# Moving one slab's skip term from TensorE to VectorE in a fused state-space and gated-FFN block, with four smaller shifts of loads and order

## The chip, the cores and the metric

One core of one Trainium2 chip runs the whole program. The metric is device time in microseconds (us) of one execution. The kernel before took 184.93 us (median of four executions beside the changed kernel, 184.4 to 185.17), a span of 183.4 us on the profile. PE is TensorE, PEld its weight loads, DVE VectorE, ACT ScalarE, POOL GpSimd, SP SyncE. L469 is line 469 of the kernel in question; the changed kernel's lines lie a few further down, so the instructions at L469 there are at L471 or so here.

## The reference

```python
xn = layernorm(x)                          # x: 2048 tokens x 512, no scale or bias
# A: diagonal state-space model, 512 complex states
Lam_bar = exp(dt * Lam);  B_bar = ((Lam_bar - 1) / Lam)[:, None] * B
h_t = Lam_bar * h_(t-1) + B_bar xn_t
y = 2 * Re(C h) + xn * Dskip               # the skip term
# B: gated FFN, F = 1376
f = (gelu(xn @ w_gate) * (xn @ w_up)) @ w_down
out = x + y * silu(f)
```

## The kernel before

The tokens are worked off in four slabs of 512 (NS = 4), each of four tiles of 128 (M = 4). Per slab, TensorE makes gate and up (eleven blocks of F), the u product of the state-space model, the down projection (`f_ps`, 11 matmuls a tile) and y (`y_ps`, 8 matmuls a tile). VectorE makes the gated products `at` (two blocks of F at a time, block 10 alone; blocks are counted from 0), the rotation by the complex phase (`pp`, `qq`, their combinations `Wt` and `hst`), the scans `Ft`, and the epilogues. The y of a slab is made during the next slab's FFN, that of the last slab at the end.

The skip term takes one of two ways. Where a tile is in `zs` (in the kernel before all tiles of slabs 1 and 2 and the first two of slab 3), VectorE makes `z = xn * Dskip` and adds it to y in the epilogue; elsewhere TensorE adds it with four small matmuls on a diagonal matrix.

```python
    def y_mm(s, m, hst):
        for h in range(2):
            flush(("h", s, h))
        y_ps = psum.tile([P, D], FP32, name="y_ps", tag="ps")
        for j in range(2 * NPT):
            nc.tensor.matmul(y_ps[:, :], lhsT=hst[:, j // NPT, j % NPT, m0 : m0 + P],
                             rhs=C2[:, j // NPT, j % NPT, :], ...)
        for kt in range(0 if (s, m) in zs else KT):          # skip term on TensorE
            nc.tensor.matmul(y_ps[:, kt * P : (kt + 1) * P], lhsT=xnT[:, kt, mg : mg + P],
                             rhs=diagI[:, kt, :], ...)
    # [...]
    def epi(s, m, y_ps, g2):
        def f():
            y = y_ps
            if (s, m) in zs:                                  # skip term on VectorE
                y = work.tile([P, D], FP32, name="yt", tag="tt", bufs=3)
                TT(out=y[:], in0=y_ps[:, :], in1=zs[s, m][:], op=ALU.add)
            TT(out=yg[:], in0=y[:, :], in1=g2[:], op=ALU.mult)
            TT(out=ot[:], in0=yg[:], in1=x_tok[:, s * M + m, :], op=ALU.add)
        dve(now() + 0.3, 1.6 if (s, m) in zs else 0.95, f)
    # [...]
    def skip(s, m, xn):
        zs[s, m] = work.tile([P, D], BF16, name="z", tag="z", bufs=9)
        dve(now() + 1.5, 0.34, lambda: TT(out=zs[s, m][:], in0=xn[:], in1=Db[:], op=ALU.mult))
```

The order of VectorE's instructions is fixed when the kernel is built, from modelled clocks: `later` puts rotation and scans in a waiting list; `dve` first takes from that list whatever the model says can still be finished in time, then emits its own instruction; `flush` takes out what a following matmul needs.

```python
    def drain(t, late):
        while waiting and max(clk["dve"], waiting[0][0]) + waiting[0][1] <= t + late:
            pop()

    def dve(ready, cost, f, late=0.8):
        drain(ready, late)
        clk["dve"] = max(clk["dve"], ready) + cost
        f()
    # [...] in ffn, after each pair of blocks:
            dve(now() + lag, 0.61, lambda: TT(out=at[:, j - 1 : j + 1, :], in0=gt[:], in1=ub[:], op=ALU.mult))
    # [...] the last slab:
    y0 = y_mm(s, 0, hsts[s])
    for m in range(M):
        g2s[s, m] = down(s, m, ats[s])
        if m == 0:
            epi(s, 0, y0, g2s[s, 0])
```

Of the kernel before, what the change touches and what calls it, by code (L numbers as in the profile page):

```python
# [19 lines left out]
def kernel(  # L20
# [70 lines left out]
    for i, v in enumerate((A_log_dt, A_Lambda_im, A_Lambda_re, A_Dskip)):  # L91
        nc.scalar.dma_start(out=pv[4 * i : 4 * i + 4, :], in_=v.rearrange("(k p) -> k p", p=P))
    CUTS = (0, 3 * P, 8 * P, F)

    def load_gu(i):
        a, b = CUTS[i], CUTS[i + 1]
        nc.sync.dma_start(out=wg[:, :, a:b], in_=wg_r[:, :, a:b])
        nc.sync.dma_start(out=wu[:, :, a:b], in_=wu_r[:, :, a:b])
# [8 lines left out]

    load_gu(0)
    load_x(1)
    load_gu(1)  # L110
    load_x(2)
    nc.sync.dma_start(out=Db[:], in_=A_Dskip.unsqueeze(0).to_broadcast([P, D]))
    for h in range(2):
        for ri, src in enumerate((A_B_re, A_B_im)):
            for pt in (h * H2, h * H2 + 1):
                nc.sync.dma_start_transpose(
                    out=BT[:, ri, :, pt * P : (pt + 1) * P], in_=src[pt * P : (pt + 1) * P, :]
                )
    load_gu(2)

# [80 lines left out]

    bn(0, 0)
    bn(0, 1)
    bn_end(0, 0)
    bn_end(0, 1)
    rstd(0, 0, 2)
    nc.gpsimd.tensor_tensor(out=dt_[:], in0=euler[:], in1=ldt, op=ALU.pow)
    bn(0, 2)
    bn(0, 3)
    xs = [norm0(0), norm0(1)]  # L210
    bn_end(0, 2)
    bn_end(0, 3)
    rstd(0, 2, 4)
    tps = [t_xn0(0, xs[0]), t_xn0(1, xs[1])]
    xnT_out(nc.vector, 0, tps[0])
    xnT_out(nc.scalar, 1, tps[1], 0, KT // 2)
    xnT_out(nc.vector, 1, tps[1], KT // 2, KT)
    xs += [norm0(2), norm0(3)]
    SPLIT = 2
    early = {}  # L220
# [15 lines left out]

    for j in range(SPLIT):
        for up in range(2):
            early[j, up] = gu_mm(0, j, up, 0, TS // 2)
        if j == 0:  # L240
            tps += [t_xn0(2, xs[2]), t_xn0(3, xs[3])]
            xnT_out(nc.scalar, 3, tps[3])
    STT(out=thn[:], in0=lim, scalar=1.0 / (2.0 * math.pi), in1=dt_[:], op0=ALU.mult, op1=ALU.mult)
# [115 lines left out]
    U0_AT = (5, 7)  # L359
    Y_AT = {1: (5, 7, 9, 10), 2: (1, 2, 3, 4), 3: (2, 4, 6, 8)}  # L360

# [141 lines left out]
    def epi(s, m, y_ps, g2):  # L503
        mg = s * TS + m * P
        yg = work.tile([P, D], BF16, name="yg", tag="yg")
        ot = work.tile([P, D], BF16, name="ot", tag="ot")

        def f():
            y = y_ps
            if (s, m) in zs:  # L510
                y = work.tile([P, D], FP32, name="yt", tag="tt", bufs=3)
                TT(out=y[:], in0=y_ps[:, :], in1=zs[s, m][:], op=ALU.add)  # L512
            TT(out=yg[:], in0=y[:, :], in1=g2[:], op=ALU.mult)  # L513
            TT(out=ot[:], in0=yg[:], in1=x_tok[:, s * M + m, :], op=ALU.add)

        dve(now() + 0.3, 1.6 if (s, m) in zs else 0.95, f)
        nc.sync.dma_start(out=out_td[mg : mg + P, :], in_=ot[:])

    def y_halves(s, m, hst, g2):
        m0 = m * P  # L520
        mg = s * TS + m0
        yg = work.tile([P, D], BF16, name="yg", tag="yg")
        ot = work.tile([P, D], BF16, name="ot", tag="ot")
        for i in range(2):
            c = slice(i * D // 2, (i + 1) * D // 2)
            y_ps = psum.tile([P, D // 2], FP32, name="y_ps", tag="ps")
            for j in range(2 * NPT):
                nc.tensor.matmul(
                    y_ps[:, :], lhsT=hst[:, j // NPT, j % NPT, m0 : m0 + P], rhs=C2[:, j // NPT, j % NPT, c],
                    start=(j == 0), stop=False,  # L530
                )
            for kt in range(KT // 2):
                k = i * (KT // 2) + kt
                nc.tensor.matmul(
                    y_ps[:, kt * P : (kt + 1) * P], lhsT=xnT[:, k, mg : mg + P], rhs=diagI[:, k, :],
                    start=False, stop=(kt == KT // 2 - 1),
                )
            TT(out=yg[:, c], in0=y_ps[:, :], in1=g2[:, c], op=ALU.mult)
            TT(out=ot[:, c], in0=yg[:, c], in1=x_tok[:, s * M + m, c], op=ALU.add)
            (nc.sync, nc.scalar)[i].dma_start(out=out_td[mg : mg + P, c], in_=ot[:, c])  # L540
# [28 lines left out]
    def skip(s, m, xn):  # L569
        zs[s, m] = work.tile([P, D], BF16, name="z", tag="z", bufs=9)  # L570
        dve(now() + 1.5, 0.34, lambda: TT(out=zs[s, m][:], in0=xn[:], in1=Db[:], op=ALU.mult))  # L571

# [8 lines left out]

    clk["pe"] = 8.1
    clk["dve"] = 10.3
    hsts, ats, g2s = {0: hst0}, {0: at0}, {}
# [18 lines left out]
    ln_vector_small(1)  # L603
    dve(13.0, 2.8, lambda: ln_vector(2))
    later(14.0, 1.2, lambda: TT(out=v4(t2_[:]), in0=v4(sa[:]), in1=sB, op=ALU.mult))
    later(14.0, 1.2, lambda: TT(out=v4(t1_[:]), in0=v4(ca[:]), in1=cB, op=ALU.mult))
# [5 lines left out]
    for s in range(NS):  # L612
        for j in range(NFT):
            ffn(s, j, ats[s])
            if s == 0:
# [9 lines left out]
                if j == 2 + M:  # L625
# [6 lines left out]
                    load_c(1)  # L632
                    load_x(3)
                if j in U0_AT:
                    chain(0, U0_AT.index(j), u_pair(0, U0_AT.index(j)), hst0)
            else:
                if j in Y_AT[s]:
                    m = Y_AT[s].index(j)
                    epi(s - 1, m, y_mm(s - 1, m, hsts[s - 1]), g2s[s - 1, m])
                if s < NS - 1 and 1 <= j < 1 + M:  # L640
                    ln_out(s + 1, j - 1)
        if s < NS - 1:
# [13 lines left out]
    s = NS - 1  # L656
    y0 = y_mm(s, 0, hsts[s])
    for m in range(M):
        g2s[s, m] = down(s, m, ats[s])
        if m == 0:  # L660
            epi(s, 0, y0, g2s[s, 0])
    for m in range(1, M - 1):
# [32 lines left out]
```

## Time and profile before

| | kernel before |
|---|---|
| device time | 184.93 us |
| span in the profile | 183.4 us |
| TensorE busy | 177.8 us (97%) |
| VectorE busy | 163.5 us (89%) |
| granted clock of TensorE | 1.0 |

Four parts of the page answer most of the question: the busy time of each engine, the row of tenths with the granted clock, the chain of waits that ended last, and the list of what each engine waited for. From the page of the kernel before, three rows of the second part (the span in 40 slices; each digit is the busy share or the granted clock in tenths), and the chain's shares by engine:

```profile
PE   7899999999999999999999999999999999999992
DVE  4886999999997999999999999999999999996053
PEclk9999999999999999999999999999999999999999
...
PE 87%; DMA 4%; DVE 4%; ACT 2%; SPq 1%; issue 0%; DVEq 0%
```

TensorE has no gap worth naming after its start, and never loses its clock there. VectorE has hardly more between slice 5 and slice 36. The busy time by stage says how few (the view of windows of the kernel before: window, length, then busy time and number of instructions of each engine, and the mean granted clock):

```profile
core 0: us, PE busy (x) PEld busy (x) DVE busy (x) ACT busy (x) POOL busy (x), PEclk, DMA share, GB/s
...
15.40:161.50 146.10, 145.95 (x688) 67.04 (x687) 143.06 (x205) 99.90 (x173) 11.18 (x23) 1.00 0.24 53
161.50:169.00 7.50, 7.50 (x36) 3.55 (x35) 6.27 (x12) 3.46 (x5) 0.00 (x0) 1.00 0.09 29
```

In the 146 us of the main part TensorE is busy for 145.95 and VectorE for 143.06.

### The profile page before, as it was taken

How to read it: one execution, taken by the hardware profiler on the slowest of the kernel's cores; microseconds unless marked ns; L12 is line 12 of the kernel's file. 1: busy time of each engine (PE TensorE's matmuls, PEld its weight loads, DVE VectorE, ACT ScalarE, POOL GpSimd, SP SyncE). 2: the span in 40 equal slices, each digit the busy share in tenths (PEclk: the TensorE clock that was granted, in tenths of full speed). 3: DMA queues.
4: the chain of work that ended last, by engine and by line, in shares of the span. 5: the costliest groups of instructions: out<-in, count | busy, mean ns of one | idle time of the engine just before them, and what ended most of it. 6: DMA issues, size and time to landing. Idle time of an engine off the chain costs nothing.

```text
span 183.4 us, 2452 instructions
## 1 busy us (share of the span) xinstructions
PE 177.8 (97%) x863; PEld 83.7 (46%) x863; DVE 163.5 (89%) x258; ACT 112.8 (62%) x196; POOL 19.9 (11%) x44
## 2 busy tenths in 40 slices
PE   7899999999999999999999999999999999999992
PEld 2474444544444444544444444444444444454451
DVE  4886999999997999999999999999999999996053
ACT  3189997678899855257789665667529444371210
POOL 3667601800000000000003000000000000000000
PEclk9999999999999999999999999999999999999999
DMA  5999695596001410010000132200000000000002
GB/s 147 309 373 120 110 225 108 129 301 168 3 0 29 80 35 32 0 45 12 0 4 0 32 84 57 57 5 0 0 0 0 0 32 29 0 30 29 29 4 86
DMA packets 24588, 12.39 MB, mean 68 GB/s; under 512 B 15776, under 2 KB 24576, under 8 KB 24576
## 3 DMA queue, kind: packets, MB, share of 16 engines
q1 hardware_dynamic: 24400, 12.16, 27.9%
q8 instruction: 7, 0.11, 0.3%
q10 hardware_dynamic: 176, 0.07, 0.1%
q14 instruction: 5, 0.04, 0.1%
HBM read 6.46 MB, written 2.10 MB: 47 GB/s over the span
## 4 chain that ended last, share of the span: by engine, by line
PE 87%; DMA 4%; DVE 4%; ACT 2%; SPq 1%; issue 0%; DVEq 0%
PE f_ps L476 21%; PE up_ps L230 19%; PE g_ps L230 19%; PE u_ps L375 15%; PE y_ps L491 13%; DMA wu<-in_B_w_up_dram 3%; DMA out_dram<-ot 1%; ACT gt L463 1%; ACT ub L464 1%; ACT xn L575 1%; DVE hst L395 1%; SPq L90 1%; DVE qq L391 1%; PE y_ps L496 0%; DVE z L571 0%; DVE yg L513 0%
## 5 line engine op out<-in xcount | busy, mean ns | idle before, releaser
L230 PE MATMUL g_ps<-xnT,wg 128*128 128x512 bf16 (+2 forms) x184 | 45.6, 370 | 0.5 <-ACT xnT L198 0.5
L230 PE MATMUL up_ps<-xnT,wu 128*128 128x512 bf16 (+2 forms) x184 | 45.5, 370 | 0.3 <-DMA wu<-in_B_w_up_dram 0.3
L463 ACT ACTIVATE gt<-g_ps 128x512 bf16<-128x512 f32 (+1 forms) x44 | 26.9, 611 | 21.1 <-PE g_ps L230 21.0
L476 PE MATMUL f_ps<-wd,at 128*128 128x512 bf16 (+1 forms) x176 | 38.7, 379 | 0.0
L464 ACT ACTIVATE ub<-up_ps 128x512 bf16<-128x512 f32 (+1 forms) x44 | 27.0, 614 | 8.0 <-PE up_ps L230 8.0
L421 DVE TENSOR_TENSOR_SCAN Ft<-rho,it,Wt 128x512 bf16<-128x512 f32 x24 | 29.6, 1269 | 0.0
L491 PE MATMUL y_ps<-C,hst 128*128 128x512 bf16 x120 | 28.4, 379 | 0.1
L375 PE MATMUL u_ps<-xnT,BT 128*128 128x512 bf16 x128 | 28.4, 379 | 0.0
L230 PEld LDWEIGHTS <-wu 128*128 128x128 bf16 (+1 forms) x184 | 18.3, 100 | 20.1 <-DMA wu<-in_B_w_up_dram 0.6
L230 PEld LDWEIGHTS <-wg 128*128 128x128 bf16 (+1 forms) x184 | 18.2, 100 | 19.5 <-issue 0.5
L476 PEld LDWEIGHTS <-at 128*128 128x128 bf16 (+1 forms) x176 | 17.2, 98 | 20.9
L380 ACT ACTIVATE U<-u_ps 128x512 bf16<-128x512 f32 x32 | 19.0, 614 | 8.6 <-PE u_ps L375 8.2
L481 ACT ACTIVATE g<-f_ps 128x512 f32<-128x512 f32 x16 | 9.6, 597 | 16.3 <-PE f_ps L476 16.3
L375 PEld LDWEIGHTS <-BT 128*128 128x128 bf16 x128 | 12.5, 98 | 14.8
L491 PEld LDWEIGHTS <-hst 128*128 128x128 bf16 x120 | 11.6, 98 | 14.5 <-DVE hst L395 0.6
L469 DVE TENSOR_TENSOR at<-gt,ub 128x1024 bf16<-128x1024 bf16 x20 | 13.5, 676 | 0.0
L512 DVE TENSOR_TENSOR yt<-y_ps,z 128x512 f32<-128x512 f32 x10 | 6.8, 680 | 7.1 <-PE y_ps L491 7.1
L157 DVE BATCH_NORM_STATS2 st<-x_tok 128x6 f32<-128x512 bf16 x12 | 7.5, 682 | 4.0 <-DMA x_tok<-in_A_x_dram 3.9
L395 DVE TENSOR_TENSOR hst<-pp,qq 128x1024 bf16<-128x1024 bf16 x16 | 10.6, 687 | 0.2
L395 DVE TENSOR_TENSOR Wt<-pp,qq 128x1024 bf16<-128x1024 bf16 x16 | 10.4, 685 | 0.2
L575 ACT ACTIVATE xn<-x_tok,nb,rs 128x512 bf16<-128x512 bf16 x12 | 10.3, 856 | 0.0
L391 DVE TENSOR_TENSOR pp<-U,cos_b 128x2048 bf16<-128x2048 bf16 x8 | 9.8, 1223 | 0.4
(109 smaller groups left out, 155.7 us busy)
## 6 DMA issues: line engine op xcount, KB each, us to landing
out_dram<-ot SPq DMA_DIRECT2D x15, 128.0 KB, 1.7
x_tok<-in_A_x_dram SPq DMA_DIRECT2D x3, 512.0 KB, 7.3
wd<-in_B_w_down_dram SPq DMA_DIRECT2D x1, 1280.0 KB
wg<-in_B_w_gate_dram SPq DMA_DIRECT2D x1, 640.0 KB
wu<-in_B_w_up_dram SPq DMA_DIRECT2D x1, 640.0 KB, 9.6
wg<-in_B_w_gate_dram SPq DMA_DIRECT2D x1, 384.0 KB, 4.4
wu<-in_B_w_up_dram SPq DMA_DIRECT2D x1, 384.0 KB
wg<-in_B_w_gate_dram SPq DMA_DIRECT2D x1, 352.0 KB
```

The costliest lines, as they stand in the source:

```text
L230: nc.tensor.matmul(ps[:fs, a:b], lhsT=w[:, kt, fsl], rhs=xnT[:, kt, s * TS + a : s * TS + b], start=(kt == 0), stop=(kt == KT - 1),)
L375: nc.tensor.matmul(u_ps[:, :], lhsT=BT[:, ri, kt, pt * P : (pt + 1) * P], rhs=xnT[:, kt, cols], start=(kt == 0), stop=(kt == KT - 1),)
L380: ACT(out=U[:, ri, q, :], in_=u_ps[:, :], func=AF.Copy)
L391: TT(out=box[key][:], in0=src()[:], in1=tab[:, hs, :].unsqueeze(1).to_broadcast(W), op=ALU.mult)
L395: return lambda: TT(out=dst()[i], in0=box["pp"][:, i, :, :], in1=box["qq"][:, 1 - i, :, :], op=op)
L421: nc.vector.tensor_tensor_scan(out=box["F"][:, ri, q, :], data0=rho[:, pt : pt + 1].to_broadcast([P, TS]), data1=box["W"][:, ri, q, :], in ...
L463: ACT(out=gt[:fs, i, :], in_=g_ps[:fs, :], func=AF.Gelu_apprx_tanh)
L464: ACT(out=ub[:fs, i, :], in_=u_ps[:fs, :], func=AF.Copy)
L469: dve(now() + lag, 0.61, lambda: TT(out=at[:, j - 1 : j + 1, :], in0=gt[:], in1=ub[:], op=ALU.mult))
L476: nc.tensor.matmul(f_ps[:, :], lhsT=at[:fs, k, m0 : m0 + P], rhs=wd[:fs, k, :], start=(k == 0), stop=(k == NFT - 1))
L491: nc.tensor.matmul(y_ps[:, :], lhsT=hst[:, j // NPT, j % NPT, m0 : m0 + P], rhs=C2[:, j // NPT, j % NPT, :], start=(j == 0), stop=((s, m) ...
L575: ACT(out=xn[:], in_=x_tok[:, s * M + m, :], func=AF.Identity, scale=rs[:, s, m : m + 1], bias=nb[:, s, m : m + 1])
```

## The change

The intent is to take sixteen small matmuls (the skip term of slab 0) off TensorE, the engine with 97%. Their z has no room of its own, so it is kept in the part of `x_tok` where the last slab's x will be, and that x is loaded later. With it come a start with norms one by one and weights in four loads instead of three, y of slabs 0 and 1 a step later, a third buffer for the output tile, and y of the last slab's first tile behind the third down projection rather than ahead of the first.

```diff
-    CUTS = (0, 3 * P, 8 * P, F)
+    CUTS = (0, 2 * P, 5 * P, 8 * P, F)
@@ loads
     load_gu(0)
+    load_gu(1)
     load_x(1)
-    load_gu(1)
+    load_gu(2)
     load_x(2)
@@ start: statistics, norms and copies of slab 0
-    bn(0, 0)
-    bn(0, 1)
-    bn_end(0, 0)
-    bn_end(0, 1)
-    rstd(0, 0, 2)
+    for m in range(2):
+        bn(0, m)
+        bn_end(0, m)
+        rstd(0, m, m + 1)
     [...]
-    xnT_out(nc.vector, 0, tps[0])
+    xnT_out(nc.scalar, 0, tps[0])
     [...]
-    SPLIT = 2
+    SPLIT = 3
@@ when y and the next x's norm are made
-    Y_AT = {1: (5, 7, 9, 10), 2: (1, 2, 3, 4), 3: (2, 4, 6, 8)}
+    Y_AT = {1: (6, 8, 9, 10), 2: (2, 3, 4, 5), 3: (2, 4, 6, 8)}
+    XN_AT = {1: 1, 2: 2}
@@ epi, y_halves
-        ot = work.tile([P, D], BF16, name="ot", tag="ot")
+        ot = work.tile([P, D], BF16, name="ot", tag="ot", bufs=3)
@@ skip
-        zs[s, m] = work.tile([P, D], BF16, name="z", tag="z", bufs=9)
+        if s == 0:
+            z = x_tok[:, (NS - 1) * M + m, :]
+        else:
+            z = work.tile([P, D], BF16, name="z", tag="z", bufs=9)[:]
+        zs[s, m] = z
@@ after the statistics of slab 2
+    for m in range(M):
+        skip(0, m, xs[m])
@@ main loop
-                    load_x(3)
     [...]
+        if s == 1:
+            load_x(3)
@@ last slab
-    y0 = y_mm(s, 0, hsts[s])
     for m in range(M):
         g2s[s, m] = down(s, m, ats[s])
-        if m == 0:
-            epi(s, 0, y0, g2s[s, 0])
+        if m == 2:
+            epi(s, 0, y_mm(s, 0, hsts[s]), g2s[s, 0])
```

More of the change, by code (lines that the diff above doesn't have):

```diff
@@ L118 @@
                 )
-    load_gu(2)
+    load_gu(3)
     warm = work.tile([P, TS], BF16, name="warm", tag="yg")
@@ L200, in xnT_out @@
             eng.tensor_copy(out=o, in_=tp[:, k0:k1, :])
-    bn(0, 0)
-    bn(0, 1)
-    bn_end(0, 0)
-    bn_end(0, 1)
-    rstd(0, 0, 2)
+    for m in range(2):
+        bn(0, m)
+        bn_end(0, m)
+        rstd(0, m, m + 1)
     nc.gpsimd.tensor_tensor(out=dt_[:], in0=euler[:], in1=ldt, op=ALU.pow)
-    bn(0, 2)
-    bn(0, 3)
-    xs = [norm0(0), norm0(1)]
+    xs = []
+    for m in range(2):
+        xs.append(norm0(m))
+        bn(0, m + 2)
     bn_end(0, 2)
@@ L239 @@
             early[j, up] = gu_mm(0, j, up, 0, TS // 2)
-        if j == 0:
-            tps += [t_xn0(2, xs[2]), t_xn0(3, xs[3])]
-            xnT_out(nc.scalar, 3, tps[3])
+            if j == 2 and up == 0:
+                tps += [t_xn0(2, xs[2]), t_xn0(3, xs[3])]
+                xnT_out(nc.scalar, 3, tps[3])
     STT(out=thn[:], in0=lim, scalar=1.0 / (2.0 * math.pi), in1=dt_[:], op0=ALU.mult, op1=ALU.mult)
@@ L511, in f @@
                 y = work.tile([P, D], FP32, name="yt", tag="tt", bufs=3)
-                TT(out=y[:], in0=y_ps[:, :], in1=zs[s, m][:], op=ALU.add)
+                TT(out=y[:], in0=y_ps[:, :], in1=zs[s, m], op=ALU.add)
             TT(out=yg[:], in0=y[:, :], in1=g2[:], op=ALU.mult)
@@ L522, in y_halves @@
         yg = work.tile([P, D], BF16, name="yg", tag="yg")
-        ot = work.tile([P, D], BF16, name="ot", tag="ot")
+        ot = work.tile([P, D], BF16, name="ot", tag="ot", bufs=3)
         for i in range(2):
@@ L569, in skip @@
     def skip(s, m, xn):
-        zs[s, m] = work.tile([P, D], BF16, name="z", tag="z", bufs=9)
-        dve(now() + 1.5, 0.34, lambda: TT(out=zs[s, m][:], in0=xn[:], in1=Db[:], op=ALU.mult))
+        if s == 0:
[3 more added lines that the diff above has]
+        zs[s, m] = z
+        dve(now() + 1.5, 0.34, lambda: TT(out=z, in0=xn[:], in1=Db[:], op=ALU.mult))
     def ln_out(s, m):
@@ L579, in ln_out @@
             skip(s, m, xn)
-    clk["pe"] = 8.1
-    clk["dve"] = 10.3
+    clk["pe"] = 7.9
+    clk["dve"] = 10.6
     hsts, ats, g2s = {0: hst0}, {0: at0}, {}
@@ L639 @@
                     epi(s - 1, m, y_mm(s - 1, m, hsts[s - 1]), g2s[s - 1, m])
-                if s < NS - 1 and 1 <= j < 1 + M:
-                    ln_out(s + 1, j - 1)
+                if s < NS - 1 and XN_AT[s] <= j < XN_AT[s] + M:
+                    ln_out(s + 1, j - XN_AT[s])
+        if s == 1:
+            load_x(3)
         if s < NS - 1:
```

## The prediction

> **What bounds the kernel now.** I read the page first, then the list of waits, then TensorE's and VectorE's timelines side by side. The page's first part gives busy time, share of the span and instructions:
>
> ```profile
> PE 177.8 (97%) x863; PEld 83.7 (46%) x863; DVE 163.5 (89%) x258; ACT 112.8 (62%) x196; POOL 19.9 (11%) x44
> ```
>
> TensorE looks like the bound, but a busy matmul is no proof. The start-to-start times say more: sixteen 128x512 matmuls of the u product take 3.45 us (22.56 minus 19.11), 0.2158 us each, and this pace holds from 12.20 us to the end. TensorE's whole list of waits is three lines:
>
> ```profile
> PE w_ps L149 <- DVE halfpi L125: 1.2, 1, 1.2
> PE g_ps L230 <- ACT xnT L198: 0.5, 1, 0.5
> PE up_ps L230 <- DMA wu<-in_B_w_up_dram: 0.3, 1, 0.3
> ```
>
> So hardly anything but matmuls is on the path. VectorE's 89% hides more: nearly all its idle time is in the first 15 us and the last 15. Its waits, of which these three of eight matter:
>
> ```profile
> DVE yt L512 <- PE y_ps L491: 7.1, 1, 7.1
> DVE st L157 <- DMA x_tok<-in_A_x_dram: 3.9, 2, 2.1
> DVE z L571 <- ACT xn L575: 1.0, 1, 1.0
> ```
>
> The 7.1 us lie in the tail, at 168.9 to 176.0. The longest single wait for x, 2.1, ends at 15.36 us, when the x of slab 2 lands. Between 15.36 and 166 us VectorE idles only the 1.0 us before a z. **Two engines are full at once**, and VectorE is the one without a reserve. Where they meet is the last slab. Its timeline (start, duration, engine, line):
>
> ```profile
> 161.51 0.68 DVE L469 TENSOR_TENSOR at<-gt,ub 128x1024 bf16<-128x1024 bf16 x1
> 162.11 1.29 DVE L395 TENSOR_TENSOR hst<-pp,qq 128x1024 bf16<-128x1024 bf16 x2
> 163.31 0.69 DVE L512 TENSOR_TENSOR yt<-y_ps,z 128x512 f32<-128x512 f32 x1
> ...
> 164.55 9.67 PE L476 MATMUL f_ps<-wd,at 128*128 128x512 bf16 x44
> ...
> 165.10 0.69 DVE L469 TENSOR_TENSOR at<-gt,ub 128x1024 bf16<-128x1024 bf16 x1
> 165.70 0.42 DVE L467 TENSOR_TENSOR at<-gt,ub 96x512 bf16<-96x512 bf16 x1
> ```
>
> The down projection begins at 164.55 and reads the ninth block of `at` after eight matmuls, at 164.55 + 8 x 0.2158 = 166.28. The product that makes blocks 8 and 9 ends at 165.10 + 0.69 = 165.79. The eleventh block is needed at 166.71 and is there at 166.12. The margin is half a microsecond, and this instruction has been ready since ScalarE's last `ub` of the pair (161.29 + 0.60): VectorE runs three microseconds behind.
>
> **What the Trainium skill says.** "TensorE: Matmul & The Clock Gate", section "Wait — 56ns, not 53.3ns?", gives N/2.4 GHz plus 2.5 ns between warm matmuls, 215.7 ns for 512 columns; the trace's 0.2158 us agrees. Its section "What's actually happening" says that after an idle window of some 3.4 us the array falls to half clock; the trace of before has no such idle stretch, and its granted clock is full all along. "VectorE: DVE Perf Modes", section "Why PSUM operands drop a tier", says that a PSUM operand in fp32 runs at the plain rate; the trace agrees: z (bf16 from SBUF) starts 0.34 us before its follower (61.95 to 62.29), yt (PSUM, fp32) 0.72 (101.81 to 102.53). "DMA: Bandwidth & Descriptors", section "Specifications", puts the least size for line rate at 512 B. The first gate weights go to exactly 512 B a row (256 columns of two bytes), so I charge no more than a little for it; no run yet shows it.
>
> **The change part by part.**
>
> Removed from TensorE: four groups of four 128x128 skip matmuls. The y of slab 0 shows one group's cost: 69.26 - 69.04 = 0.22 us on the path. 4 x 0.22 = **0.88 us**.
>
> Added to VectorE: four z products, 4 x 0.34 = 1.36 us, directly after the statistics of slab 2, and four adds that put z to y, 4 x 0.72 = 2.88 us. Sum **4.24 us**, all in the stretch in which it has no idle time. What can swallow it is only the 1.04 us idle before z in slab 1.
>
> The start: the transposes follow the 14 warm-up matmuls (the last group starts at 5.25 and they are at 6.62), so norms one by one can't bring them forward. Before, the gate product at 7.70 had to be followed by the up product at 8.69, when its weights landed. A first load of two thirds should land a third sooner in its own time, 8.64 less some 1.3 us, which closes that 0.5 us hole. Against it: the second pair of transposes now stands one matmul group before its readers rather than two, and copying to SBUF took 10.38 - 9.13 = 1.25 us from the first transpose, with 0.44 us of matmuls between; and six PSUM banks instead of four are held early, so TensorE may wait for ScalarE's first gelu. I put the start at -0.3 to +0.4 us.
>
> y a step later: TensorE lost about 0.32 us in slab 1's first y (2.21 us for eight matmuls where others take 1.89), waiting for hst. A step is 1.73 us; VectorE is later by 1.36 - 1.04 + one z (0.34), so at most 0.3 us is won.
>
> The last slab: y of tile 0 (8 x 0.2158 = 1.73 us) moves behind the third down projection. It moves the start of the down projection forward. And the order of the instructions in the changed kernel shows VectorE making blocks 8 and 9 after the last y of slab 2 and pp, block 10 after qq; hst follows them.
>
> The end: a third ot buffer takes away the 0.46 us wait of the last but one output for an old store; 0.2 to 0.3 us of it reach the end.
>
> **The sum.** If TensorE stayed the bound: 0.88 + 0.2 + 0.25 = 1.3 us less, 183.7. I do not believe it, because of the last slab.
>
> VectorE's side: from 15.36 to 166.12 it took 150.76 us, of which 1.04 were idle: 149.7 of work up to block 10. In the changed kernel 4.24 more and two hst combinations less (162.11 to 163.31, 1.2), so 152.7; plus some 0.3 us idle before the second z of slab 1's x, which ScalarE gives at 21.05. The x of slab 2 has the same bytes ahead of it in the queue as before, in more descriptors; I add 0.2. Block 10 is there at 15.36 + 0.2 + 152.7 + 0.3 = **168.6 us**, blocks 8 and 9 some 1.4 us before that (qq and overlap between), near 167.3.
>
> TensorE's side: 164.55 - 1.73 - 0.88 - 0.2 + 0.3 (start) = 162.0 for the down projection; it needs block 8 at 163.8. So it waits about **3.5 us for blocks 8 and 9 and 1 us for block 10**, in all some 4.4 us.
>
> From block 10 on: 34 down matmuls and 24 of y, 58 x 0.2158 = 12.52, the skip of one whole y 0.22, the last y in halves 1.74 + 0.22: 14.7 us. 168.7 + 14.7 + 0.2 for the pipeline = 183.6 for the last matmul, where before was 179.9 (179.59 + 0.28). The tail was 183.4 - 179.9 = 3.5 and becomes 3.3: a span of 186.9. The device time was 1.6 over the span (185.01 - 183.4): **188.6 us, 1.9% slower**.
>
> **The rivals.** (1) TensorE stays the bound and the change wins 1 to 1.5 us: 183.5 to 184. For it speaks that matmuls really go away; against it the half microsecond of margin above, and that nothing before the last slab lets VectorE catch up: TensorE isn't stopped by it earlier (hst and at of slabs 1 and 2 have one to three microseconds to spare by the same sum). (2) The wait comes and the array's clock falls as well: a gap near 3.5 us is about the skill's window. Half pace for about 3.4 us would cost about 1.7 us more: 190.3. For it, the length of the gap; against it, that two matmuls break it up. (3) Loads in smaller pieces push slab 2's x or the weights back; every 0.5 us at x is 0.5 us at the end, as VectorE has nothing else to do there: 189. Against it: equal bytes, and rows no smaller than 512 B. (4) The reload of slab 3's x comes late, because its room holds z until the last y of slab 0 (near 80 us). It is needed near 88 (the statistics on ScalarE). Such a load took 7.3 us in the median, behind other loads; the queue is nearly empty there, so it should be hidden.
>
> **Range and chances.** Without the fall of the clock 188.6 give or take 0.7; with it (three in ten) 190.3; a wrong sum for VectorE (one in eight) would give anything from 183.7 to 187. The line of 2% is 188.7, inside my range, so the verdict is a toss-up: same 0.50, slower 0.48, faster 0.02. Range 186.4 to 190.6; I name 188.7.
>
> **What would show it.** Right: TensorE's list of waits gains f_ps <- VectorE's at, 3 to 5 us, all near 163 to 169 us; VectorE's busy time rises by 4.2 us; the z wait on xn in slab 1 shrinks; the 7 us idle of yt in the tail splits up. Step by step: sixteen skip matmuls fewer; blocks 8 to 10 ready at 167 to 169. The clock row shows whether rival 2 came. Wrong: no such wait, or VectorE's other durations changed, or x of slab 2 landing well before or after 15.5 us, or a large new wait in slab 0 or 1.

## The result, and the profile after

| | before | changed |
|---|---|---|
| device time, median of four | 184.93 us | 190.43 us (190.26 to 191.62) |
| span in the profile | 183.4 us | 188.3 us |
| VectorE busy | 163.5 us | 167.5 us |
| waits of TensorE for `at` | none | 3.07 and 0.86 us |
| granted clock, four executions | 1.0 (the profiled one) | 0.991, 0.982, 0.991, 0.991 |

The ratio is 1.0315 with a 95% interval of 1.0267 to 1.0363: slower. A ratio here is the mean time of one kernel's fast runs over the mean of the other's fast runs of the same rounds, so it is not quite the ratio of the medians. All executions told of below were marked fast (none was over 1.5% above the fastest of its kernel) and all kernels gave correct results.

From the page of the changed kernel, the row of the clock, the chain's shares by engine, and the busy times:

```profile
PE 178.6 (95%) x855; PEld 83.9 (45%) x855; DVE 167.5 (89%) x266; ACT 113.1 (60%) x197; POOL 19.5 (10%) x45
...
PEclk9999999999999999999999999999999999987999
...
DVE 73%; PE 9%; ACT 6%; DMA 4%; SPq 4%; issue 3%; DVEq 0%
```

The chain has changed hands: 87% TensorE before, 73% VectorE now. The clock row has a dent near its end. TensorE's waits (engine, what it waited for, total, times, longest):

```profile
PE f_ps L478 <- DVE at L471: 3.1, 1, 3.1
...
PE f_ps L478 <- DVE at L469: 0.9, 1, 0.9
```

The two `f_ps` waits are new. The last slab's timeline shows both, and what VectorE did meanwhile (start, duration, engine, line; the idle time before in brackets):

```profile
161.84 1.89 PE L478 MATMUL f_ps<-wd,at 128*128 128x512 bf16 x8
163.15 0.67 DVE L514 TENSOR_TENSOR yt<-y_ps,z 128x512 f32<-128x512 f32 x1
...
164.92 1.22 DVE L393 TENSOR_TENSOR pp<-Ft,cos_b 128x2048 bf16<-128x2048 bf16 x1
166.05 0.68 DVE L471 TENSOR_TENSOR at<-gt,ub 128x1024 bf16<-128x1024 bf16 x1
166.66 1.22 DVE L393 TENSOR_TENSOR qq<-Ft,sin_b 128x2048 bf16<-128x2048 bf16 x1
166.79 0.60 PE L478 MATMUL f_ps<-wd,at 128*128 128x512 bf16 x2 [3.07 <-DVE at L471]
167.79 0.42 DVE L469 TENSOR_TENSOR at<-gt,ub 96x512 bf16<-96x512 bf16 x1
168.26 6.83 PE L478 MATMUL f_ps<-wd,at 96*128 96x512 bf16 x23 [0.86 <-DVE at L469]
168.66 0.15 PEld L478 LDWEIGHTS <-at 128*128 128x128 bf16 x1 [0.27 <-issue]
169.08 0.15 PEld L478 LDWEIGHTS <-at 128*128 128x128 bf16 x1 [0.28 <-issue]
...
171.64 2.95 PEld L478 LDWEIGHTS <-at 128*128 128x128 bf16 x14 [0.28 <-issue]
```

TensorE starts the down projection at 161.84, 2.7 us earlier than before (164.55), and stands at its ninth matmul until blocks 8 and 9 are there at 166.73. Just before that VectorE did an epilogue of slab 2 (`yt` and two more) and `pp`, neither of which TensorE needed yet. From 168.26 on, weight loads come every 0.43 us instead of every 0.216: half pace, until 171.64. The windows of the changed kernel put numbers to it:

```profile
15.40:161.50 146.10, 145.70 (x676) 66.57 (x675) 143.53 (x211) 100.94 (x175) 11.40 (x26) 1.00 0.24 53
161.50:169.00 7.50, 3.57 (x15) 1.20 (x14) 7.43 (x11) 2.24 (x4) 0.00 (x0) 0.95 0.05 17
...
169.00:172.50 3.50, 3.50 (x11) 1.35 (x10) 0.41 (x1) 0.50 (x1) 0.00 (x0) 0.61 0.00 0
```

In 161.5 to 169 us TensorE is busy for 3.57 us where it was 7.50, and VectorE for 7.43 where it was 6.27. The last row, 0.61 of full clock, is read as "busy" all through: a busy TensorE is not one at its peak.

### The profile page after: what moved, and what is told of

It reads as the page before. It is cut to its first block, busy times and chain, and to the rows that moved or that the text cites. A ratio compares the mean times of both kernels' runs of the same rounds, so it can differ in the third digit from the quotient of the medians.

```text
span 188.3 us, 2444 instructions
## 1 busy us (share of the span) xinstructions
PE 178.6 (95%) x855; PEld 83.9 (45%) x855; DVE 167.5 (89%) x266; ACT 113.1 (60%) x197; POOL 19.5 (10%) x45
## 4 chain that ended last, share of the span: by engine, by line
DVE 73%; PE 9%; ACT 6%; DMA 4%; SPq 4%; issue 3%; DVEq 0%
DVE Ft L423 18%; DVE qq L393 10%; DVE pp L393 9%; DVE at L471 5%; DVE Wt L397 5%; PE f_ps L478 5%; DVE hst L397 5%; DVE yg L515 4%; DMA x_tok<-in_A_x_dram 4%; DVE yt L514 4%; PE y_ps L493 3%; DVE ot L516 3%; SPq L98 2%; ACT ub L466 2%; DVE z L578 2%
## 5 line engine op out<-in xcount | busy, mean ns | idle before, releaser
L478 PE MATMUL f_ps<-wd,at 128*128 128x512 bf16 (+1 forms) x176 | 40.9, 391 | 3.9 <-DVE at L471 3.1
L231 PEld LDWEIGHTS <-wg 128*128 128x128 bf16 (+1 forms) x188 | 18.7, 100 | 20.2 <-issue 1.0
L515 DVE TENSOR_TENSOR yg<-yt,g 128x512 bf16<-128x512 f32 x14 | 9.7, 692 | 0.6
```

The costliest lines, as they stand in the source:

```text
L231: nc.tensor.matmul(ps[:fs, a:b], lhsT=w[:, kt, fsl], rhs=xnT[:, kt, s * TS + a : s * TS + b], start=(kt == 0), stop=(kt == KT - 1),)
L478: nc.tensor.matmul(f_ps[:, :], lhsT=at[:fs, k, m0 : m0 + P], rhs=wd[:fs, k, :], start=(k == 0), stop=(k == NFT - 1))
```

## The experiments

Twelve kernels ran, each timed in the same rounds as the kernel before. Its medians were 185.22 us for e1 to e4, 185.07 for e5 to e8, 184.83 for e9 to e11 and 185.03 for e12. The changed kernel itself was timed only in its own rounds (184.93 us for the kernel before), so each comparison with its 190.43 us below is one across rounds, and the 0.4 us between these medians is the noise to allow for.

**The theory.** (T1) VectorE has 4.2 us more to do ahead of the last products of `at`, so TensorE waits in the last slab; (T2) the wait takes TensorE's clock, which costs on top. **Rivals.** (R1) The cost comes from another part of the change, the start, the later y or the moved y of tile 0. (R2) The clock fall is only a by-product and costs nothing by itself. (R3) Not the amount of VectorE's work but its order decides.

### e1: the change without the skip term

```diff
-    for m in range(M):
-        skip(0, m, xs[m])
```

> The changed kernel without its first part: the four z of slab 0 and their four adds are gone from VectorE, the sixteen skip matmuls of slab 0 are back on TensorE (0.88 us); start, loads, y a step later and the late y of tile 0 stay. Theory (VectorE overbooked by 4.24 us, TensorE waits for at in the last slab, and its clock falls): block 10 of at is ready near 166 instead of 168.2, the wait before f_ps shrinks from 3.9 us to some 1.3 us, too short for the clock to fall, granted clock 1.00, time 185.5 to 186.5. Rival (the loads in four pieces, the norms or the late y cost the time): it stays near 190.

Measured: 187.25 us (186.76 to 187.49), ratio 1.0098 (1.0064 to 1.0132). The skip term accounts for 3.2 us of the 5.5. But the run is slower than expected, and 1% slower than before, which could be a share of R1. Its profile has TensorE waiting less than 1 us for `at`:

```profile
166.73 3.64 PE L478 MATMUL f_ps<-wd,at 128*128 128x512 bf16 x16 [0.76 <-DVE at L471]
```

Two things blur it. Its start was late (the first transposes at 7.08 us rather than 6.03), and with less work in the model the generator also reorders VectorE: `qq` and both `hst` come ahead of blocks 8 and 9 here, behind them in the changed kernel. It is not the same order with less work, so its 2 us over the kernel before can't be divided between R1 and R3; e4, which contains every part that R1 names, is no slower than the kernel before.

### e2: the skip term alone, on the kernel before

```diff
+        if s == 0:
+            z = x_tok[:, (NS - 1) * M + m, :]
+    [...]
+    for m in range(M):
+        skip(0, m, xs[m])
     [...]
-                    load_x(3)
+        if s == 1:
+            load_x(3)
```

> The kernel before with the first part alone (slab 0's z in the room of slab 3's x, that x loaded after slab 1's y); y not a step later, y of tile 0 of slab 3 still ahead of the down projection. Theory: VectorE is as late as in the changed kernel, and TensorE now also waits for hst where the changed kernel gave it a step more: some 2 us at the first y of slab 1, 5 us or more at y of tile 0 in the last slab, and the clock falls after it: 190 to 193 us, no better than the changed kernel. Rival (loads or norms at fault): 184 to 185.

Measured: 192.83 us (192.27 to 193.1), ratio 1.0404 (1.0373 to 1.0436), as expected. By itself the skip term is dearer than the whole change. The late work now shows as one wait for `hst`, because y of tile 0 still stands ahead of the down projection:

```profile
169.22 2.74 PE L491 MATMUL y_ps<-C,hst 128*128 128x512 bf16 x6 [5.29 <-DVE hst L395]
```

T1 is supported. The other parts of the change gain something on net when they come with the skip term, against R1 in its plain form. The trace shows one of these gains: at the first y of slab 1, which here stands where the kernel before has it, TensorE waits 1.75 us for `hst`, against 0.40 us in the changed kernel with that y a step later.

### e3: the changed kernel with TensorE kept busy in its wait

```diff
+        if m == 0:
+            fill = psum.tile([P, TS], FP32, name="fill", tag="ps")
+            for _ in range(14):
+                nc.tensor.matmul(fill[:, :], lhsT=xnT[:, 0, 0:P], rhs=xnT[:, 0, 0:TS], start=True, stop=True)
         g2s[s, m] = down(s, m, ats[s])
```

> The changed kernel with fourteen matmuls into an unused PSUM tile ahead of the last slab's first down projection: 14 x 0.2158 = 3.0 us of TensorE work inside a wait of 4.3 us, so that the wait for at is the same and only the idle time goes. Theory (idle time lowers the clock, which costs 1.7 to 1.9 us beside the wait itself): block 10 of at as late as ever (168.2 us), clock 1.00 throughout, time near 188.5. Rival (the slow stretch after the wait has another cause, such as the weights or PSUM): stays at 190.4 or grows.

Measured: 189.15 us (188.87 to 189.59), ratio 1.0212 (1.018 to 1.0243). Fourteen useless matmuls make the kernel 1.3 us faster. Its clock is 0.998 to 1.0 in all four executions. The filler takes the room of the first wait; the second stays, and so does VectorE's lateness:

```profile
162.16 3.19 PE L671 MATMUL fill<-xnT 128*128 128x512 bf16 x14
...
168.59 5.14 PE L478 MATMUL f_ps<-wd,at 96*128 96x512 bf16 x23 [0.86 <-DVE at L469]
```

It resumes at 168.59, 0.33 us later than the changed kernel did, and still ends 1.4 us sooner: last matmul at 183.21 + 0.28 = 183.49 rather than 184.57 + 0.28 = 184.85. R2 falls. From resuming to the end of the last matmul are 14.90 us here and 16.59 in the changed kernel: the clock fall costs **1.69 us**.

### e4: the changed kernel with the products of `at` first

The products of blocks 8 to 10 are emitted ahead of the waiting list in the last slab, one scan is taken out before block 10, and the epilogue of slab 2's last tile is held until after them. VectorE does the same work, in another order.

```diff
+        late = -99.0 if s == NS - 1 and j >= NFT - 2 else 0.8
+        if s == NS - 1 and j == NFT - 1:
+            pop()
     [...]
-            dve(now() + lag, 0.61, lambda: TT(out=at[...], ...))
+            dve(now() + lag, 0.61, lambda: TT(out=at[...], ...), late)
     [...]
-                    epi(s - 1, m, y_mm(s - 1, m, hsts[s - 1]), g2s[s - 1, m])
+                    y = y_mm(s - 1, m, hsts[s - 1])
+                    if s == NS - 1 and m == M - 1:
+                        held = y
+                    else:
+                        epi(s - 1, m, y, g2s[s - 1, m])
     [...]
     s = NS - 1
+    epi(s - 1, M - 1, held, g2s[s - 1, M - 1])
```

> The changed kernel with VectorE's order changed in the last slab alone: the products of at for blocks 8 to 10 ahead of the epilogue of slab 2's last y, of one scan and of pp and qq. VectorE does the same work. Theory: blocks 8 and 9 at 161.7, block 10 at 163.2, no wait before the down projection, clock 1.00; hst at 169.1 to 169.7 is just in time for y of tile 0; all of the gain of 1.2 us that was hoped for appears: 183.4 to 184.4 us. Rival (VectorE's total work is the bound, its order is of no use): 187 or more.

Measured: 184.74 us (184.4 to 185.23), ratio 0.9973 (0.9943 to 1.0004), a little above the expected range, and 5.7 us below the changed kernel. VectorE is as busy as there (167.8 us). The three lines to compare with those of the changed kernel:

```profile
160.38 1.44 DVE L474 TENSOR_TENSOR at<-gt,ub 128x1024 bf16<-128x1024 bf16 x2
162.02 7.30 PE L481 MATMUL f_ps<-wd,at 128*128 128x512 bf16 x32
162.93 0.40 DVE L472 TENSOR_TENSOR at<-gt,ub 96x512 bf16<-96x512 bf16 x1
```

Blocks 8 and 9 are done near 161.8 instead of 166.73, TensorE runs on, and the clock is 0.998 to 1.0. So the added work alone is not the cause; the added work at the place in the order where it delays the products is. T1 needs R3 with it. The work moved behind them (an epilogue, a scan, `pp`, `qq`, `hst`) still comes in time for the y that needs it, since that y stands behind the third down projection.

### e5: the start alone, on the kernel before

The edit is the first three groups of the diff above (cuts and order of loads, start, SPLIT) and the two modelled start times.

> The kernel before with only the start of the change: norms of slab 0 one by one, gate and up weights in four loads, three blocks split, the modelled clocks of the start. The u product began 0.35 us earlier in the changed kernel, but VectorE from the landing of slab 2's x on is the bound and that landing does not move. My theory: within 0.3 us of before, 184.7 to 185.5, TensorE's waits below 2 us, VectorE busy as before (163.5). Rival: TensorE is the bound and the earlier start counts in full, 184.5 to 184.8. Rival of a hidden cost of the start (smaller loads, banks held): 185.8 or more, with a new wait of TensorE in the first 20 us.

Measured: 185.78 us (185.34 to 185.96), ratio 1.0039 (1.0019 to 1.0059): 0.7 us slower, above what I expected. From the first transposes to the u product are 12.49 us in the kernel before (6.62 to 19.11), but 12.73 in this run (6.71 to 19.44), in the changed kernel (6.03 to 18.76) and in e1, e6, e9 and e12 alike. With the old start and no weight load in the way it is 12.22 us (e2: 6.69 to 18.91; e10: 6.55 to 18.77). So the new start costs 0.24 to 0.51 us. TensorE's list names where: the copy of tile 0's transposes, now on ScalarE, is waited for twice (0.74 and 0.25 us), against 0.47 and then 0.28 for a weight load in the kernel before:

```profile
PE g_ps L231 <- ACT xnT L199: 1.0, 2, 0.7
```

The changed kernel's u product began 0.35 us earlier than before only because its transposes happened to begin 0.59 us earlier. That point varies from execution to execution: 6.03 to 7.10 us over the profiles of runs with this same start, with the same five warm-up matmuls before it taking 1.25 to 2.02 us. It goes with the moment at which the traces' record of the granted clock first shows full clock: 4.47 us in the changed kernel's profile, 5.86 in that of the kernel before, 6.83 in e9's.

### e6: the skip term of two tiles instead of four

```diff
-    for m in range(M):
+    for m in range(2):
         skip(0, m, xs[m])
```

> The changed kernel with z on VectorE for two of the four tiles of slab 0 (the other two keep their skip matmuls). VectorE carries 2 x (0.34 + 0.72) = 2.1 us less. My theory of a threshold: blocks 8 to 10 come 2 us earlier (block 10 near 166.2), TensorE waits 1.5 to 2.2 us rather than 4.0 and its clock does not fall: 186.2 to 187.2. Rival, each skip product costs the same whatever its number: half way between 185.0 and 190.4, 187.7. Rival, the skip products are not the cause but where the second y of slab 0 falls: above 189.

Measured: 191.45 us (190.03 to 191.98), ratio 1.0337 (1.0293 to 1.0381). My expectation was wrong by more than 4 us: half of the added work, and no gain. The timeline shows why; VectorE's order is not the same:

```profile
164.63 1.22 DVE L393 TENSOR_TENSOR qq<-Ft,sin_b 128x2048 bf16<-128x2048 bf16 x1
165.77 0.69 DVE L471 TENSOR_TENSOR at<-gt,ub 128x1024 bf16<-128x1024 bf16 x1
166.37 1.29 DVE L397 TENSOR_TENSOR hst<-pp,qq 128x1024 bf16<-128x1024 bf16 x2
...
167.57 0.41 DVE L469 TENSOR_TENSOR at<-gt,ub 96x512 bf16<-96x512 bf16 x1
```

With less modelled work `drain` finds room for `qq` ahead of blocks 8 and 9 and for `hst` ahead of block 10: 1.2 + 1.2 us of work that TensorE doesn't wait for, in place of the 2.1 us saved. Block 10 is ready at 167.98, hardly before the 168.21 of the changed kernel. The clock falls here too (0.991, 0.982, 0.982, 0.982; 0.982 is about twice the loss of 0.991, so three executions lost some 1.7 us more than the profiled one). This speaks for R3 and makes e6 worthless as a measure of T1's amount; e9 mends that.

### e7: all z products on GpSimd

```diff
-        dve(now() + 1.5, 0.34, lambda: TT(out=z, in0=xn[:], in1=Db[:], op=ALU.mult))
+        dve(now() + 1.5, 0.34, lambda: nc.gpsimd.tensor_tensor(out=z, in0=xn[:], in1=Db[:], op=ALU.mult))
```

> The changed kernel with all fourteen z products on GpSimd, the order of everything else on VectorE kept. VectorE carries 14 x 0.34 = 4.8 us less. My theory (only the amount of work ahead of blocks 8 to 10 counts): these blocks come 4 us or more earlier, the wait for them is gone, 183.5 to 184.5. Rival: GpSimd and VectorE hold up each other when both read two operands from SBUF, so that GpSimd's z takes several times 0.34 us and VectorE's instructions beside it grow; then VectorE's busy time falls by less than 3 us and the time is 185.5 to 190.

Measured: 196.93 us (196.26 to 197.13), ratio 1.0639 (1.0615 to 1.0664): the rival came, and worse than I had it. By lines, a z takes 1.4 to 1.6 us on GpSimd (0.42 on VectorE), and VectorE, rid of fourteen instructions, is busy for longer than in the changed kernel (173.6 us against 167.5). From the groups of lines (count, busy us, mean ns of one, then the idle time before):

```profile
L471 DVE TENSOR_TENSOR at<-gt,ub 128x1024 bf16<-128x1024 bf16 x20 | 16.0, 801 | 1.0 <-ACT ub L466 1.0
L578 POOL TENSOR_TENSOR z<-xn,Db 128x512 bf16<-128x512 bf16 x10 | 15.6, 1578 | 17.2 <-ACT xn L582 17.2
```

The same `at` product takes 677 ns on average in the changed kernel and 801 here. The Trainium skill has it in "SBUF — State Buffer", section "SBUF: two separate sides": the port pair of VectorE and GpSimd is "an exclusive lock, not a bandwidth split", and a VectorE instruction with two SBUF inputs is among those that take it against a GpSimd one. The trace agrees in kind: seventeen of the twenty `at` products take 0.66 to 0.70 us as ever, and the three that take 1.26, 1.57 and 1.64 us run beside z products on GpSimd, as does a 128x4 product that takes 1.15 us (0.16 in the kernel before). Not all beside a z grow: one `at` product at 59.85 us takes 0.67. GpSimd idles for 90% of the changed kernel, and still is no place for this work.

### e8: y of tile 0 back ahead of the last down projection

```diff
+    y0 = y_mm(s, 0, hsts[s])
     for m in range(M):
         g2s[s, m] = down(s, m, ats[s])
-        if m == 2:
-            epi(s, 0, y_mm(s, 0, hsts[s]), g2s[s, 0])
+        if m == 0:
+            epi(s, 0, y0, g2s[s, 0])
```

> The changed kernel with y of the last slab's tile 0 put back ahead of the down projection, where before has it. The combinations hst end at 169.4 us there, so TensorE waits some 6 us in one piece ahead of y instead of 4.0 in two, and does 32 down matmuls less while it waits. My theory: 191.5 to 193, one wait y_ps<-hst of 5 to 7 us, clock fall as well: the late y is a part of the change that gains. Rival: where TensorE does the 1.73 us of y is indifferent because VectorE sets the time: 190 to 191.

Measured: 192.75 us (192.06 to 193.7), ratio 1.0419 (1.0374 to 1.0464), as expected. TensorE's wait is one of 6.43 us for `hst`, and the clock 0.978 to 0.982. The late y is a part of the change that helps: about 2 us (2.3 by the medians), by giving TensorE three tiles of down projection (33 matmuls) to do that need no `hst`. It may also be most of why e2 was slower than the whole change.

### e9: two tiles, with VectorE's order kept

As e6, but for the two tiles left the modelled clocks of both engines are advanced as if z and its add were there.

```diff
-        pe_takes(2 * NPT + ((s, m) not in zs))
+        pe_takes(2 * NPT + (s == NS - 1 and m >= 2))
     [...]
+        else:
+            dve(now() + 1.5, 0.34, lambda: None)
     [...]
-        dve(now() + 0.3, 1.6 if (s, m) in zs else 0.95, f)
+        dve(now() + 0.3, 1.6 if (s, m) in zs or s == 0 else 0.95, f)
```

> As the run with two skip tiles, but the bookkeeping of the modelled clocks is left as in the changed kernel, so VectorE has the same order of instructions with 2.1 us less work. There, the lighter model let qq and hst slip ahead of the products of blocks 8 to 10, which ate the gain. My theory (amount of work ahead of these products, at a fixed order): blocks 8 and 9 near 164.6, block 10 near 166.1, TensorE waits 1.5 to 2 us and keeps its clock: 186.0 to 187.0. Rival, that the two tiles left cost as much as four for another reason than order: 189.5 or more.

Measured: 187.73 us (187.65 to 188.53), ratio 1.0151 (1.0126 to 1.0175), clock 1.0 in all four. At a fixed order, half the work costs 2.9 us where the whole costs 5.5, and the clock, which held, is 1.7 of the difference. But it is 0.7 us above my range, and the profiled execution (188.53, the slowest) shows block 10 at 168.14, only 0.07 us earlier than in the changed kernel. Two lines of VectorE's list account for most of the 2.1 us saved:

```profile
DVE z L578 <- ACT xn L582: 1.2, 1, 1.2
...
DVE at L471 <- ACT ub L466: 1.0, 1, 1.0
```

Near 20 and 22 us it now waits for ScalarE, 1.25 + 0.97 us, where the changed kernel waited 0.60. With another 0.33 us in the third slab that is 1.95 us more idle time. TensorE had started late in this execution (transposes at 7.10), so VectorE ran into it: where both engines are full, relieving one makes it wait for the other. The other three executions have spans 0.8 us shorter; the profile shows only this one.

It is also the cleanest measure of the clock. TensorE resumes at 168.20, almost exactly where the changed kernel does (168.26), after waits of 1.49 and 0.86 us at full clock, and its last matmul ends at 182.82 + 0.28 = 183.10: 14.90 us later, as in e3, not 16.59.

### e10: a version meant to beat both

The changed kernel with e4's order, the start of the kernel before, and a new tail: for the last two tiles z times g2 plus x is made in VectorE's idle time, so that they need no skip matmuls and their last epilogues keep two operations. As no tile needs the diagonal matrix any more, the four ScalarE instructions that build it (`skip_diag`, 1.5 us) go too.

```diff
+    def skip_late(s, m):
+        zs[s, m] = z = work.tile([P, D], BF16, name="zl", tag="z", bufs=9)[:]
+        TT(out=z, in0=xns[s, m][:], in1=Db[:], op=ALU.mult)
+        TT(out=z, in0=z, in1=g2s[s, m][:], op=ALU.mult)
+        TT(out=z, in0=z, in1=x_tok[:, s * M + m, :], op=ALU.add)
+        ws[s, m] = z                                # the epilogue: ot = y * g2 + ws
     [...]
+        if m >= 2:
+            skip_late(s, m)
```

> A version meant to beat both: the changed kernel with the products of blocks 8 to 10 first, the start of the kernel before (its norms, loads and split: 0.24 us less from the first transposes to the u product), and the last two tiles' skip taken off TensorE too: z times g2 plus x is made in VectorE's idle time of the tail, so that the last epilogues keep two operations. Skip matmuls off the last tiles: 2 x 0.22 us on the path. 184.74 less 0.24 less 0.44 gives 184.05: 183.6 to 184.6. Rival: VectorE's last instructions set the end, and the three extra operations a tile delay them: 184.7 or more.

Measured: 184.07 us (183.82 to 184.39, six executions), ratio 0.9955 (0.9936 to 0.9973), as expected. It beats the kernel before by 0.45%, the changed one by some 6 us. TensorE's whole list of waits is two lines, both of the start (1.2 us for `halfpi`, 0.5 us for `xnT`), as before without the one for a weight load.

### e11: the new tail alone, on the kernel before

The edit is `skip_late` of e10 without the rest.

> The kernel before with only the tail's new epilogue (z times g2 plus x ahead of time, no skip matmul in the last two tiles). If the tail's matmuls are on the path, 0.44 us less than before. Rival: no gain or a loss, as VectorE's waits for g of the last tile move its epilogues back.

Measured: 184.94 us (184.53 to 186.31), ratio 1.0009 (0.998 to 1.0037): no gain that can be seen. In the trace TensorE does end 0.87 us earlier, of which 0.43 is a u product that began earlier (18.68 instead of 19.11) and 0.44 the eight small matmuls; but VectorE then waits 0.42 us for the store of an old output tile, a wait that a third buffer removes in e10. So I can't say what part of e10's gain the tail has.

### e12: five fillers instead of fourteen

The edit is e3's with `range(5)`.

> The changed kernel with 5 instead of 14 filler matmuls ahead of the last down projection (1.08 us). VectorE's products come as late as before, so the idle time of TensorE falls from 3.07 + 0.86 to about 2.0 + 0.86 us. Runs so far: 1.49 + 0.86 kept the full clock, 2.46 + 0.93 lost it. If an idle length between decides, 188.5 to 189.3 at clock 0.997 or more when it is held; if not, 190.0 or more at clock 0.991 or less as in the changed kernel. Both tell where the limit lies; nothing else should differ.

Measured: 189.63 us (189.49 to 190.57), ratio 1.0264 (1.0231 to 1.0298). Three executions kept the clock (1.0: 189.49, 189.69, 189.58), one did not (0.991: 190.57). The profiled one waited 1.99 and 0.86 us at full clock, and its 14.90 us from resuming (169.16) to the last matmul's end (184.06) agree with e3 and e9. It resumed late because its transposes had begun at 6.92. The limit runs through this kernel (waits and idle time are those of the profiled execution alone, the first clock of each row; the last column is explained below):

| run | waits in the last slab | granted clock of four executions | most idle time in one cell |
|---|---|---|---|
| e9 | 1.49 and 0.86 us | 1.0, 1.0, 1.0, 1.0 | 1.48 us |
| e12 | 1.99 and 0.86 us | 1.0, 0.991, 1.0, 1.0 | 1.65 us |
| e7 | 2.83 and 0.86 us | full there in the profiled one; it fell at another place | 1.90 us |
| e6 | 2.46 and 0.93 us | 0.991, 0.982, 0.982, 0.982 | 2.02 us |
| changed | 3.07 and 0.86 us | 0.991, 0.982, 0.991, 0.991 | 2.76 us |

The length of the wait alone is no sharp limit. The profiled execution of e7 waited longer than e6's and kept its clock in the last slab (175.30 to the last matmul's end at 190.19 are 14.89 us). It lost it in slab 1, after a wait of 4.46 us there.

The Trainium skill, "TensorE: Matmul & The Clock Gate", section "What's actually happening", says that activity is watched in windows of 3413 ns that run free of the kernel. The traces agree. Each holds a record of the granted clock. In all fourteen, full clock lasts a whole number of 3.413 us from its first rise to its first fall (48 in the changed kernel and e6, 18 in e7), and a half-clock stretch that ends within the kernel lasts one or two. So the first rise fixes a grid of cells, in which TensorE's busy time, as the profile models it, can be read; the rest of a cell is called idle here. The changed kernel's cell before its fall and the cell after it, e6's before its fall, and the two emptiest of e7's last slab (the clock is the third figure from the end):

```profile
164.90:168.31 3.41, 0.65 (x3) 0.16 (x4) 3.41 (x6) 0.00 (x0) 0.00 (x0) 1.00 0.11 38
168.31:171.72 3.41, 3.41 (x9) 1.21 (x10) 1.10 (x2) 0.60 (x1) 0.00 (x0) 0.50 0.00 0
...
165.42:168.83 3.41, 1.39 (x6) 0.52 (x7) 2.57 (x5) 0.36 (x1) 0.00 (x0) 1.00 0.11 38
...
169.48:172.89 3.41, 1.51 (x8) 0.49 (x5) 3.34 (x5) 1.76 (x2) 0.00 (x0) 1.00 0.00 0
172.89:176.31 3.42, 1.62 (x7) 0.62 (x8) 3.42 (x6) 0.59 (x1) 0.00 (x0) 1.00 0.11 38
```

In all fourteen profiles, after the start, a full-clock cell idle for 2.01 us or more is followed by half clock (the least are 2.01 in e8's tail and 2.02 in e6), and none idle for 1.92 us or less is (1.92 in e10, 1.90 in e7). e7's waits fell on two cells, 1.90 and 1.79 us, and neither was enough; that they did looks like chance, as the grid lies differently in each profile (first rise at 4.47 to 6.83 us). My estimate from these figures, with a limit of 2 us and the grid anywhere: waits as long as the changed kernel's lose the clock at nearly every position of the grid, e12's at about half of them, e9's at about a third. One cell at half pace costs half of 3.413 us, 1.71, close to the 1.69 measured.

## Why the prediction was right or wrong

- **Bound and the wait: right.** VectorE was the engine without a reserve. Its busy time rose by 4.0 us (predicted 4.2); block 10 came at 168.21 (168.6); blocks 8 and 9 at 166.73 (near 167.3); TensorE waited 3.07 + 0.86 us (3.5 + 1); the down projection began at 161.84 (162.0).
- **The time without a clock fall: right.** Predicted 188.6. The changed kernel's 190.43 less the 1.69 us of the fall is 188.7. From resuming to the last matmul's end the prediction had 14.7 + 0.2 us; e3, e9 and e12 show 14.90. That the total agrees to a tenth is partly luck: TensorE resumed 0.4 us earlier than reckoned, while the tail was some 0.2 us and the device time over the span 0.4 us longer (3.5 and 2.0 us, not 3.3 and 1.6). The sum has a slip, too: it carries block 10 on as 168.7 after finding 168.6, and adds up to 188.5, not 188.6.
- **The step that failed: TensorE's work after the wait was reckoned at full clock.** The fall was only rival 2, put at three in ten, with "that two matmuls break it up" against it. All four executions of the changed kernel lost clock (0.991 or 0.982), and the two matmuls (0.43 us of work) did not save it: the cell of 3.41 us before the fall was idle for 2.76, and 2.01 was enough elsewhere. Its size was right: 1.7 us predicted, 1.69 measured. With it the rival's own 190.3 stands beside 190.43; the prediction named 188.7, the time without the fall.
- **Rival 1** (TensorE stays the bound, a gain): fell, and e4 shows when it would have held: with the products first. Even then the gain is 0.5 us, with an interval that touches zero, not 1.3.
- **Rivals 3 and 4** (loads): neither showed. x of slab 2 was there for the statistics at 15.41 us (15.36 before); the reload of slab 3's x went out at 81.05 and no engine's list has a wait for it.
- **The later y and the end**: the prediction gave `hst` of slab 1 one to three microseconds to spare, and it had none. The first y of slab 1 still waits 0.40 us for it (0.32 before), so nothing was won against the kernel before; but with the skip term and without the later place it was 1.75 us (e2). At the end, the 0.46 us wait for an old output store is gone.
- **The start**, put at -0.3 to +0.4 us: the 0.24 us of the trace are inside, the 0.51 us against e2 and e10 and the 0.7 us of e5's device time are not. I had hoped for a gain from the hole closed at the up product, and there is a loss: the hole before the gate product grew by more, since the copy moved to ScalarE.
- **What I did not see** is how the order came about. I took it from the changed kernel as given, and reckoned with the amount of work alone. e1, e4 and e6 show the order at least as strong: e4, same work, is 5.7 us faster; e6, half of the added work, is no faster. The products of `at` were queued behind work with a later reader.
- **Not settled**: what the later y of slabs 0 and 1 is worth in time (no run has it alone; e2's trace shows only the wait that it shortens), and why the clock's limit lies near 2 us of idle time in 3.41.

## What to carry to other kernels

Before moving work off the busiest engine, look how many microseconds the receiving engine idles in the stage concerned, not in the whole; and when it is full, ask which of its results the other engine reads first, and emit those first: here the order in one place was worth 5.7 us (1.7 of them the clock's), more than all the work moved. When an order comes out of a cost model, any edit that changes the modelled work changes the order too, so pin the order in an experiment that is to measure the work. Where new waits of TensorE can add up to two microseconds within 3.41, count a possible clock fall too: in these profiles it came with 2.01 us idle in one cell and not with 1.92. Independent useful work in program order ahead of a wait shortens it (e8: the late y is worth some 2 us); useless matmuls inside it, as in e3, only keep the clock.

## What the Trainium skill lacked or had wrong

- "TensorE: Matmul & The Clock Gate", section "Why this matters for your kernels", advises no idle gaps above some 3 us, and puts the fall down to a window of idle time. Here no single gap needed to be that long: a gap of 2.46 us, two matmuls and another of 0.93 us took the clock, with 1.39 us of work in the cell of 3.41 us. Over fourteen profiles, cells idle for 2.01 us or more lost the clock and cells idle for 1.92 us or less kept it. The page gives no such share.
- "GPSIMD Engine Reference", section "Engine selection", puts a two-input elementwise operation on GpSimd at about twice VectorE's time. Here a 128x512 bf16 product took 1.4 to 1.6 us on average beside a busy VectorE, against 0.42 us on VectorE, which is 3.3 to 3.8 times; and three of VectorE's own twenty 128x1024 products grew from 0.68 to 1.26, 1.57 and 1.64 us, which that comparison doesn't count.
